# Reordering the start of a linear-attention and bilinear-FFN kernel: unit 0 finished ahead of unit 1, the first up tile by channel tiles, units 2 and 3 one up tile later

## Chip, cores and metric

The kernel runs on one core of a Trainium2 chip. The metric is the device time of one execution in microseconds (us), the median of several runs. Engines are named as in the profile: PE (matrix multiplications), DVE (vector engine), ACT (scalar engine), POOL (GpSimd), and SP, which only issues DMAs here.

## What is computed

A gated linear attention for 4 batches of 8 heads, 768 tokens and 48 channels a head, and behind it a bilinear feed-forward layer on the 3072 tokens of 384 channels:

```python
f = 1.0 / (1.0 + np.exp(-f_logit))
for t in range(S):
    state = f[:, :, t, :, None] * state + np.einsum('bhd,bhe->bhde', k[:, :, t], v[:, :, t])
    y[:, :, t] = np.einsum('bhd,bhde->bhe', q[:, :, t], state)
x = y.transpose(0, 2, 1, 3).reshape(B * S, H * D)
out = ((x @ w_a) * (x @ w_b)) @ w_out          # 384 -> 1536 -> 384
```

## The kernel before

Tokens are cut into 8 blocks of 384 (`BLK`), two a batch. A block's attention is done in two **units** of four heads each; units 0 and 1 (`FIRST`) belong to block 0, units 2 and 3 to block 1, and so on up to 15. What a unit yields goes by DMA into `xT[blk]`, which holds the block's 384 channels as three channel tiles of 128: unit 0 fills channels 0 to 191 (tile 0 and half of tile 1), unit 1 the rest.

A unit runs through these steps, each a function:

- `front_parts(u)` (L313): part 0 is two sigmoids on ACT and one operation on POOL; part 1 two long scans (`scan_f`) and a small `hold` on DVE; part 2 a reciprocal and six short scans (`scan_inv`) on DVE; part 3 the products with `k` and `q` (`times`) on DVE.
- `turn` (transposes of k on PE), `turned` (copies to SBUF on ACT), `scores` (PE), `mask` (DVE), `within` (PE), `gains` (PE), `carried` (five or six small additions on DVE, which make the states `st`), `across` (PE, with the states).
- `out_of_bank` (three copies out of PSUM: part 0 has 128 rows, parts 1 and 2 have 48), `stored` (five DMAs into `xT`), and, for a first half of a batch, `hand_on` (scales the last state for the next block).

Behind that stands the feed-forward layer. For the first two blocks it is done in **up tiles**: `up(blk, ft)` (L598) makes columns 128·ft to 128·ft+127 of both products, b and a, with three matmuls each (one for each channel tile, `kt`), b first, into two of the four PSUM banks `ps_f`; `product` (L624) copies b on ACT and multiplies on DVE into `groups`, which gives the banks back. 12 up tiles a block, 24 in all.

The weights come as 64-bit floats and are converted on the chip in 20 **pieces**: pieces 0 and 1 are w_b and w_a for up tile 0; 2 and 3 those for tiles 1 and 2; 4 and 5 for 3 and 4; 6 and 7 for 5 and 6; 8 and 9 for 7 and 8. A piece costs two ACT operations and one on POOL (`begin`, first half: L71, L72, L73), one more on ACT (`begin`, second half: L75) and, in `end`, one DVE shift (L78) and three DVE additions (L83), one for each channel tile. `begin(9.5)` means: the first half of piece 9 too.

`keep_up(n)` (L1002) issues n matmuls whose result nobody reads.

The order of the work on each engine is written out by hand from L1014 to L1132; behind it a loop runs up tiles alone (L1140), and from L1150 on a planner places everything by estimated costs. [...] Around the change, in the kernel before:

- units 0 and 1 are interleaved: both fronts, then `mask(0)`, `scores(1)`, `within(0)`, `mask(1)`, `within(1)`, then `across(0)`, `across(1)` and the copies of both, and only then the ten DMAs into `xT[0]` (L1062 to L1068). Unit 0's go over SP; of unit 1's, three go over ACT's queue and two over POOL's (L565).
- `keep_up(6)`, `up(0, 0)`, then `turn(2)` and `scores(2)`, `up(0, 1)`, `within(2)`, `gains(2)`, `up(0, 2)`, `across(2)`, `up(0, 3)`, `turn(3)`, `scores(3)`, `up(0, 4)`, `within(3)`, `gains(3)`, `up(0, 5)`, `across(3)`, `y_of(3)`.
- then `ups`: (0, 6), (0, 7), then tiles of block 1 and block 0 in turn. 13 of the remaining 18 run in the loop (`alone`), 5 in the planner's part.
- unit 2's scans and products (L1071, L1082) stand on DVE before pieces 2 and 3, piece 8 is begun and ended before `across(3)`; piece 9 is begun before it, both halves, and ended on DVE in the loop, just ahead of `up(0, 7)`, which needs it.

Of the kernel before, what the change touches and what calls it, by code (L numbers as in the profile page):

```python
# [22 lines left out]
BLK = 384  # L23
# [130 lines left out]
def by_quotients(ctx, tc, q, k, f_logit, v, moe_w_a, moe_w_b, moe_w_out, out, ident, weights, bad, ps_f):  # L154
# [117 lines left out]
    def begin(n):  # L272

        while 2 * n > begun[0] < 2 * len(todo):
            i, second = divmod(begun[0], 2)
            dst, src, shape = todo[i]
            if not second:
                going.append(
                    from_double(
                        nc, dst, raws[i], shape[0], next(blocks), bits[i % len(bits)], some, whole, shape[0] == NKT  # L280
                    )
                    if src.dtype != FP32 else iter(())
                )
            next(going[i], None)
            begun[0] += 1
# [71 lines left out]
            [(DVE, 880, times, "k", inv), (DVE, 880, times, "q", F)],  # L357
        )

    def front(u):  # L360

        for part in front_parts(u):
            for _, _, do, *args in part:
                do(*args)
            yield

    ps_x, ps_y = (ps_a.tile([128, 2, 512], FP32, tag=n, name=n) for n in ("ps_x", "ps_y"))
    idle = list(range(4))

# [113 lines left out]
    def hand_on(u):  # L483

        if unit(u)[1] == NH - 1:
            return
        before = live[u]["st"][-1]
        for n in range(2):
            end = products_of_f[u][:, n, BLK - 1:BLK]
            nc.vector.tensor_scalar(before[:, n], before[:, n], end, math.exp(-MIDDLE), ALU.mult, ALU.mult)  # L490
# [44 lines left out]

    def out_of_bank(u, part):

        if not part:
            if u == NQ - 1:

                live[u]["y_sb"] = groups[:, 2 * NTG - 1, PIECE:].rearrange("r (o p m) -> r o p m", p=2, m=SUB)
            else:
                live[u]["y_sb"] = sb1.tile([128, 2 * NC, 2, SUB], FP32, tag="y", name="y")
        p, e, r, rows = ((0, 0, 0, 128), (1, R, 0, D), (1, 0, R, D))[part]
        copy = nc.vector.tensor_copy if u == NQ - 1 and p else nc.scalar.copy
        copy(live[u]["y_sb"][r:r + rows, :, p], live[u]["y"][p][e:e + rows, 0:BLK].rearrange("r (o m) -> r o m", m=SUB))

    def stored(u):
# [4 lines left out]
    def stores_of(u):  # L553

        b, half, qd = unit(u)
        blk = b * NH + half

        def begin():
            if qd == 0:
                xT[blk] = sb2.tile([128, NKT, BLK], FP32, tag="xT", name="xT")  # L560
            live.pop(u - NQ, None)

        def store(n, h, kt, p, row, w):
            y = live[u]["y_sb"].rearrange("r (n c) p m -> r n (c p m)", n=2)
# [24 lines left out]
    def on_pe(load, do, *args):  # L589
        beats[0] += 1  # L590
        return PE, load, 0, do, *args
# [3 lines left out]

    factors = []

    def up(blk, ft):  # L598

        for _, _, _, do, *args in up_steps(blk, ft):  # L600
            do(*args)

    def up_steps(blk, ft):

        ps = {}

        def emit(nm, w, kt):
            if kt == 0:
                ps[nm] = ps_f[idle.pop(0)]
            nc.tensor.matmul(  # L610
                ps[nm][:, 0:BLK],
                lhsT=w[:, kt, ft * 128:ft * 128 + 128],
                rhs=xT[blk][:, kt],
                start=kt == 0,
                stop=kt == NKT - 1,
            )
            if len(ps) == 2 and kt == NKT - 1:
# [368 lines left out]
    with tc.manual_schedule():  # L986
# [9 lines left out]
        fronts = {u: front(u) for u in (0, 1, 3)}  # L996

        def emit_all(steps):
            for _, _, do, *args in steps:
# [2 lines left out]
        def keep_up(n):  # L1002

            x = products_of_f[0][:, 0]
            for _ in range(n):
                nc.tensor.matmul(ps_f[idle[-1]][:, 0:BLK], lhsT=ident, rhs=x, start=True, stop=True)

        def y_of(u):
            for part in range(3):
                out_of_bank(u, part)  # L1010
            stored(u)

# [1 line left out]
        for u in FIRST:  # L1014
            load_unit(u, "f")
        for u in FIRST:
            next(fronts[u])
        patterns()
        for u in FIRST:
            load_unit(u, "k")  # L1020
# [4 lines left out]
        load_weights(2)  # L1025
        load_unit(2, "k")
        load_unit(2, "q")
        for _ in range(3):
            next(fronts[0])
        begin(1)  # L1030
        keep_up(2)
        turn(0)
        turned(0)
        scores(0)
        begin(2)
        gains(0)
        keep_up(4)
        for _ in range(3):
            next(fronts[1])
        turn(1)  # L1040
        turned(1)
        mask(0)
        scores(1)
        emit_all(front_parts(2)[0])
        begin(2.5)
        carried(0, range(4))
        within(0)
        gains(1, range(NC - 1))
        end(1)
        mask(1)  # L1050

        carried(1, range(1))
        carried(0, range(4, 5))
        _, (first_scan, *scans), *others = front_parts(2)
        emit_all([first_scan])
        within(1)
        gains(1, range(NC - 1, NC))
        across(0)
        carried(1, range(1, NJ))
        carried(0, range(5, NJ))  # L1060
        emit_all(scans)
        for u in FIRST:  # L1062
            if u:
                across(u)
            for part in range(3):
                out_of_bank(u, part)
        for u in FIRST:
            stored(u)  # L1068
        begin(3)
        end(2)  # L1070
        emit_all(others[0])  # L1071
# [8 lines left out]
        keep_up(6)  # L1080
        up(0, 0)
        emit_all(others[1])  # L1082
        begin(4)
        next(fronts[3])
        end(3)
        load_unit(3, "v")
        end(4)
        turn(2)
        scores(2)
        load_unit(4, "f")  # L1090
        up(0, 1)
        mask(2)
        for u in FIRST:
            hand_on(u)
        product()
        turned(2)
        begin(5)
        next(fronts[3])
        next(fronts[3])
        within(2)  # L1100
        gains(2)
        product()
        carried(2)
        begin(6.5)
        up(0, 2)
        across(2)
        end(6)
        next(fronts[3])
        y_of(2)
        load_weights(2)  # L1110
        product()
        begin(7.5)
        up(0, 3)
        turn(3)
        turned(3)
        scores(3)
        end(7)
        mask(3)
        product()
        begin(8)  # L1120
        up(0, 4)
        within(3)
        gains(3)
        end(8)
        carried(3)
        product()
        begin(10)
        end(9)
        up(0, 5)
        across(3)  # L1130
        y_of(3)
        product()  # L1132


        ups = [(0, 6), (0, 7)]
        for i in range(8, NFT):
            ups += [(1, i - 8), (0, i)]
        ups += [(1, i) for i in range(NFT - 8, NFT)]
        alone = len(todo) - 7
        for n, (blk, i) in enumerate(ups[0:alone]):  # L1140
            convert(needed(i))
            up(blk, i)
            end(8 + n)
# [528 lines left out]
```

## Time and profile before

| | |
|---|---|
| median of 3 runs (lowest to highest) | 596.69 us (595.27 to 597.24) |
| the profiled execution's own time, its span | 595.13 us, 593.4 us |
| PE busy, share of the span | 571.1 us, 96% |
| DVE busy | 412.1 us, 69% |
| ACT busy | 256.8 us, 43% |
| chain that ended last | PE 84%, DVE 11% |
| first matmul of any kind | 10.67 us |
| first up matmul starts; the next five of its tile start from | 31.90 us; 34.11 us |
| `across(3)` starts; the next up tile starts | 65.67 us; 66.48 us |

All places in time are counted from the start of the span. "Busy" is time in which an engine worked; what an engine's idle time costs is read from who waited for it.

### The profile page before, as it was taken

What the parts mean: (1) busy time and instruction counts of PE and PEld (TensorE: products, weight loads), DVE (VectorE), ACT (ScalarE), POOL (GpSimd) and SP (SyncE); (2) the same over time, 40 slices, a digit from 0 to 9 for tenths busy, and PEclk for the clock granted to TensorE, in tenths of its full rate; (3) what the DMA queues carried; (4) which work ended last, traced back from release to release, by engine and by line L of the source; (5) the groups of instructions that cost most, each with busy time, mean ns of one, the idle gap of its engine ahead of it and who ended that gap; (6) DMA issues with size and microseconds to landing.
All of it is one profiled execution on the core that took longest, in us unless ns stands there. A gap on an engine that the chain in (4) does not pass through costs nothing.

```text
span 593.4 us, 13932 instructions
## 1 busy us (share of the span) xinstructions
PE 571.1 (96%) x5802; PEld 511.8 (86%) x5802; DVE 412.1 (69%) x786; ACT 256.8 (43%) x487; POOL 89.0 (15%) x72
## 2 busy tenths in 40 slices
PE   2899999999999999999999999999999999999996
PEld 1655655557999999999999999999999999999996
DVE  6999445599978678958895678847785165835751
ACT  5577848653122464235521444326431335135300
POOL 7365637454000000000000000000000000000000
PEclk9999999999999999999999999999999999999999
DMA  8696689089552440044004410041001100000001
GB/s 216 183 253 207 221 263 272 0 150 186 114 144 70 115 93 11 15 119 97 2 1 127 109 22 2 2 106 42 3 1 48 48 2 0 2 28 1 0 29 32
DMA packets 33560, 49.42 MB, mean 83 GB/s; under 512 B 3984, under 2 KB 25264, under 8 KB 33488
## 3 DMA queue, kind: packets, MB, share of 16 engines
q1 hardware_dynamic: 30000, 42.19, 25.8%
q0 software_dynamic: 3056, 5.92, 5.9%
q8 instruction: 47, 0.77, 0.6%
q10 hardware_dynamic: 432, 0.34, 0.2%
q14 instruction: 25, 0.20, 0.1%
HBM read 33.23 MB, written 4.72 MB: 64 GB/s over the span
## 4 chain that ended last, share of the span: by engine, by line
PE 84%; DVE 11%; issue 2%; ACT 1%; DMA 1%; SPq 0%; DVEq 0%; ACTq 0%
PE ps_f L732 35%; PE ps_f L834 28%; PE ps_f L610 13%; PE ps_y L501 2%; DVE inv L346 2%; PE ps_y L527 2%; PE ps_x L403 2%; PE ps_x L452 1%; DVE sums L724 1%; PE ps_x L428 1%; DVE groups L724 1%; DVE w_ba L83 1%; DVE q_in L350 1%; DVE f_in L333 1%; DVE spare L346 1%
## 5 line engine op out<-in xcount | busy, mean ns | idle before, releaser
L610 PE MATMUL ps_f<-xT,w_ba 128*128 128x384 f32 x288 | 95.6, 489 | 1.5 <-DMA xT<-y 1.4
L1319 ACT COPY sums<-ps_f 128x384 f32<-128x384 f32 x120 | 57.5, 480 | 75.8 <-PE ps_f L732 62.2
L610 PEld LDWEIGHTS ps_f<-xT,w_ba 128*128 128x128 f32 x288 | 53.9, 190 | 38.2 <-issue 2.2
L1319 ACT COPY groups<-ps_f 128x384 f32<-128x384 f32 x120 | 57.8, 482 | 64.3 <-PE ps_f L732 41.9
L732 PE MATMUL ps_f<-xT,w_ba 128*128 128x192 f32 x384 | 78.3, 326 | 0.0
L732 PEld LDWEIGHTS ps_f<-xT,w_ba 128*128 128x128 f32 x384 | 64.8, 190 | 0.1
L73 POOL TENSOR_SCALAR sums<-sums 128x768 f32<-128x768 f32 (+1 forms) x20 | 52.2, 2612 | 35.8 <-ACT sums L71 35.6
L732 PE MATMUL ps_f<-groups,w_ba 128*128 128x192 f32 x288 | 55.3, 328 | 0.0
L732 PE MATMUL ps_f<-x_sums,raw 128*128 128x192 f32 x288 | 53.8, 331 | 1.1 <-DVE groups L724 0.9
L329 POOL TENSOR_SCALAR inv<-inv 128x768 f32<-128x768 f32 x14 | 12.9, 923 | 265.9 <-ACT inv L326 265.8
L834 PE MATMUL ps_f<-w_out,sums 128*128 128x192 f32 x288 | 52.1, 329 | 0.3 <-DVE groups L632 0.3
L834 PE MATMUL ps_f<-w_out,groups 128*128 128x192 f32 x288 | 51.7, 328 | 0.0
L732 PEld LDWEIGHTS ps_f<-x_sums,raw 128*128 128x128 f32 x288 | 47.0, 190 | 4.1 <-DVE groups L724 2.1
L834 PE MATMUL ps_f<-spare,sums 128*128 128x192 f32 x288 | 49.0, 326 | 0.0
L732 PEld LDWEIGHTS ps_f<-groups,w_ba 128*128 128x128 f32 x288 | 47.9, 190 | 0.5 <-ACT groups L1319 0.2
L834 PEld LDWEIGHTS ps_f<-w_out,sums 128*128 128x128 f32 x288 | 47.1, 190 | 1.0 <-DVE groups L632 0.6
L834 PEld LDWEIGHTS ps_f<-w_out,groups 128*128 128x128 f32 x288 | 47.1, 190 | 0.7
L834 PEld LDWEIGHTS ps_f<-spare,sums 128*128 128x128 f32 x288 | 47.1, 190 | 0.1
L724 DVE TENSOR_TENSOR sums<-sums,groups 128x768 f32<-128x768 f32 x36 | 34.7, 964 | 13.4 <-ACT groups L1319 13.0
L724 DVE TENSOR_TENSOR sums<-ps_f,sums 128x384 f32<-128x384 f32 x60 | 32.9, 552 | 15.9 <-PE ps_f L732 14.0
L732 PE MATMUL ps_f<-x_sums,w_ba 128*128 128x192 f32 x192 | 39.4, 328 | 0.5 <-DVE sums L724 0.5
L732 PE MATMUL ps_f<-xT,raw 128*128 128x192 f32 x192 | 39.6, 329 | 0.0
(142 smaller groups left out, 851.0 us busy)
## 6 DMA issues: line engine op xcount, KB each, us to landing
raw<-w_ba POOLq DMA_DIRECT2D x11, 512.0 KB, 8.5
k_in<-in_k_dram SPq DMA_DIRECT2D x32, 144.0 KB, 4.4
q_in<-in_q_dram SPq DMA_DIRECT2D x32, 144.0 KB, 4.3
v_in<-in_v_dram SPq DMA_DIRECT2D x16, 288.0 KB, 5.7
raw<-in_moe_w_out_dram SPq DMA_DIRECT2D x6, 768.0 KB, 5.6
out_dram<-o SPq DMA_DIRECT2D x22, 192.0 KB, 1.9
f_in<-in_f_logit_dram SPq DMA_DIRECT2D x28, 144.0 KB, 3.1
xT<-y SPq DMA_DIRECT2D x45, 72.0 KB, 2.1
```

The costliest lines, as they stand in the source:

```text
L73: nc.gpsimd.tensor_scalar(h, h, HI_MIN, HI_MAX, ALU.max, ALU.min)
L83: nc.vector.tensor_tensor(dst[:, rows], hu[:, rows], bit[:, rows], ALU.add)
L329: nc.gpsimd.tensor_scalar(inv, inv, EXP_K, 1.0, ALU.mult, ALU.add)
L346: nc.vector.tensor_tensor_scan(inv[:, w], inv[:, w], none[:, 0:C], first, ALU.mult, ALU.add)
L403: nc.tensor.matmul(ps[h][SUB * p:SUB * p + SUB, o:o + SUB], lhsT=kf[r, tokens(n, c, p)], rhs=qf[r, tokens(n, c, p)], start=True, stop=True,)
L501: nc.tensor.matmul(ps[p][e:e + D, o:o + SUB], lhsT=t["v"][r, n, c, h * D:h * D + D], rhs=at[r, h, o:o + SUB], start=o == 0, stop=True, ski ...
L527: nc.tensor.matmul(ps[p][e:e + D, o:o + SUB], lhsT=st[j][r, n], rhs=qf[r, tokens(n, c, p)], start=False, stop=True, skip_group_check=True,)
L610: nc.tensor.matmul(ps[nm][:, 0:BLK], lhsT=w[:, kt, ft * 128:ft * 128 + 128], rhs=xT[blk][:, kt], start=kt == 0, stop=kt == NKT - 1,)
L724: nc.vector.tensor_tensor(to, x, y, op)
L732: nc.tensor.matmul(ps[:, g], lhsT=sums_of_w[name][:, g, 128 * j:128 * j + 128], rhs=sums_of_x[blk][name], start=start and g == 0, stop=Tru ...
L834: nc.tensor.matmul(to, lhsT=x[:, i // 2, i % 2], rhs=w[:, NI * (i % 2) + i // 2], start=start and i == 0, stop=i == HFT - 1, skip_group_ch ...
L1319: do(*args)
```

## The change

Unit 0 is brought to its end, DMAs included, before unit 1's transposes. Unit 0's states are made between unit 1's short scans. Unit 0's and unit 1's PSUM copies run in the order part 1, part 2, part 0; of unit 1's three, one stays on DVE instead of two. Unit 1's five DMAs into `xT[0]` go round SP, ACT and POOL. `hand_on` for units 0 and 1 moves from four DVE operations to six on ACT. Two `keep_up` calls change from 4 to 3 and from 6 to 3. Up tile 0 goes by channel tiles: b and a of tile 0, then of tile 1, then of tile 2.

On DVE, pieces 2 and 3 move ahead of the second part of unit 2's front (piece 2 ahead of its scans, piece 3 between the scans and the rest). On PE, `up(0, 1)` moves ahead of `turn(2)`, and every later step of units 2 and 3 stands behind one more up tile: `across(3)` now follows `up(0, 6)`. Unit 3's DVE work moves behind `up(0, 3)`. Piece 9 is begun in halves around `y_of(3)`, and ended in the loop. The loop runs 12 up tiles and starts with (0, 7); the planner's part has the same five.

```diff
@@ hand_on
+        if u in FIRST:
+            end = sb2.tile([128, 2], FP32, tag="end", name="end")
+            nc.scalar.mul(end, products_of_f[u][:, :, BLK - 1], math.exp(-MIDDLE))
+            for n in range(2):
+                nc.scalar.mul(before[:, n], before[:, n], end[:, n:n + 1])
+            return
@@ out_of_bank
-        copy = nc.vector.tensor_copy if u == NQ - 1 and p else nc.scalar.copy
+        copy = nc.vector.tensor_copy if u == NQ - 1 and part == 1 else nc.scalar.copy
@@ stores_of
+        queues = itertools.cycle((nc.sync, nc.scalar, nc.gpsimd) if u == NQ - 1 else (nc.sync,))
...
-            queue = nc.sync if u != NQ - 1 else nc.gpsimd if n else nc.scalar
+            queue = next(queues)
@@ up_steps
-        for nm, w in (("b", w_b), ("a", w_a)):
-            for kt in range(NKT):
-                yield on_pe(BEAT, emit, nm, w, kt)
+        order = [(nm, w, kt) for nm, w in (("b", w_b), ("a", w_a)) for kt in range(NKT)]
+        for nm, w, kt in sorted(order, key=lambda x: x[2]) if by_tiles else order:
+            yield on_pe(BEAT, emit, nm, w, kt)
```

The hand-written order in the kernel after, from unit 0's scores on:

```python
        scores(0)
        *scans, hold = parts[1][1]
        emit_all(scans)
        mask(0)
        emit_all([hold])
        begin(2)
        gains(0, range(NC - 1))
        emit_all(parts[2][0])
        within(0)
        gains(0, range(NC - 1, NC))
        keep_up(3)
        for i, step in enumerate(parts[1][2]):
            emit_all([step])
            if i > 1:
                carried(0, range(i - 2, i - 1))
        across(0)
        emit_all(parts[1][3])
        turn(1)
        y_of(0)
        turned(1)
        scores(1)
        end(1)
        mask(1)
        begin(2.5)
        gains(1, range(NC - 1))
        within(1)
        gains(1, range(NC - 1, NC))
        carried(1, range(NJ - 1))
        across(1)
        y_of(1)
        for u in FIRST:
            carried(u, range(NJ - 1, NJ))
        end(2)
        begin(3)
...
        keep_up(3)
        up(0, 0, True)
        begin(4)
        end(3)
        load_unit(3, "v")
        emit_all(parts[2][1])
        end(4)
        load_unit(4, "f")
        emit_all(parts[2][2])
        emit_all(parts[2][3])
        emit_all(parts[3][0])
        up(0, 1)
        product()
        for u in FIRST:
            hand_on(u)
        begin(5)
        turn(2)
        scores(2)
        turned(2)
        up(0, 2)
        end(5)
        mask(2)
        product()
        begin(6)
        within(2)
        gains(2)
        end(6)
        up(0, 3)
...
        up(0, 6)
        product()
        carried(3)
        across(3)
        begin(9.5)
        end(9)
        y_of(3)
        begin(10)
        product()

        ups = [(0, 7), (0, 8), (1, 0), (1, 1), (1, 2)]
...
        alone = len(todo) - 8
        for n, (blk, i) in enumerate(ups[0:alone]):
            convert(needed(i))
            up(blk, i)
            end(8 + n + n // 6)
```

More of the change, by code (lines that the diff above doesn't have):

```diff
@@ L358, in front_parts @@
         )
[L360 to L365, printed above, removed]
     ps_x, ps_y = (ps_a.tile([128, 2, 512], FP32, tag=n, name=n) for n in ("ps_x", "ps_y"))
@@ L536, in out_of_bank @@
     def out_of_bank(u, part):
-        if not part:
+        if "y_sb" not in live[u]:
             if u == NQ - 1:
@@ L596, in by_quotients, with up, up_steps @@
     factors = []
-    def up(blk, ft):
-        for _, _, _, do, *args in up_steps(blk, ft):
+    def up(blk, ft, by_tiles=False):
+        for _, _, _, do, *args in up_steps(blk, ft, by_tiles):
             do(*args)
-    def up_steps(blk, ft):
+    def up_steps(blk, ft, by_tiles=False):
         ps = {}
@@ L616, in emit @@
             )
-            if len(ps) == 2 and kt == NKT - 1:
+            if nm == "a" and kt == NKT - 1:
                 factors.append((blk, ft, ps))
-        for nm, w in (("b", w_b), ("a", w_a)):
-            for kt in range(NKT):
-                yield on_pe(BEAT, emit, nm, w, kt)
+        order = [(nm, w, kt) for nm, w in (("b", w_b), ("a", w_a)) for kt in range(NKT)]
+        for nm, w, kt in sorted(order, key=lambda x: x[2]) if by_tiles else order:
+            yield on_pe(BEAT, emit, nm, w, kt)
     def product():
@@ L995, in by_quotients @@
             nc.scalar.copy(ps[:, :, 0:BLK], zero.unsqueeze(1).broadcast_to((128, 2, BLK)))
-        fronts = {u: front(u) for u in (0, 1, 3)}
+        parts = {u: front_parts(u) for u in range(2 * NQ)}
         def emit_all(steps):
@@ L1008, in y_of @@
         def y_of(u):
-            for part in range(3):
+            for part in (1, 2, 0) if u in FIRST else range(3):
                 out_of_bank(u, part)
@@ L1016, in by_quotients @@
         for u in FIRST:
-            next(fronts[u])
+            emit_all(parts[u][0])
         patterns()
@@ L1027, in by_quotients @@
         load_unit(2, "q")
-        for _ in range(3):
-            next(fronts[0])
+        for part in parts[0][1:]:
+            emit_all(part)
         begin(1)
@@ L1034, in by_quotients @@
         scores(0)
+        *scans, hold = parts[1][1]
+        emit_all(scans)
+        mask(0)
+        emit_all([hold])
         begin(2)
[L1036 to L1039, printed above, removed]
+        gains(0, range(NC - 1))
+        emit_all(parts[2][0])
+        within(0)
+        gains(0, range(NC - 1, NC))
[4 more added lines that the diff above has]
+                carried(0, range(i - 2, i - 1))
+        across(0)
+        emit_all(parts[1][3])
         turn(1)
+        y_of(0)
         turned(1)
-        mask(0)
         scores(1)
[L1044 to L1048, printed above, removed]
         end(1)
         mask(1)
[L1052 to L1055, printed above, removed]
+        begin(2.5)
+        gains(1, range(NC - 1))
         within(1)
         gains(1, range(NC - 1, NC))
[L1058 to L1061, printed above, removed]
+        carried(1, range(NJ - 1))
+        across(1)
+        y_of(1)
         for u in FIRST:
[L1063 to L1068, printed above, removed]
+            carried(u, range(NJ - 1, NJ))
+        end(2)
         begin(3)
-        end(2)
-        emit_all(others[0])
         load_unit(3, "f")
@@ L1079, in by_quotients @@
         load_unit(3, "q")
-        keep_up(6)
-        up(0, 0)
-        emit_all(others[1])
+        keep_up(3)
+        up(0, 0, True)
         begin(4)
-        next(fronts[3])
         end(3)
         load_unit(3, "v")
+        emit_all(parts[2][1])
         end(4)
+        load_unit(4, "f")
+        emit_all(parts[2][2])
+        emit_all(parts[2][3])
+        emit_all(parts[3][0])
+        up(0, 1)
+        product()
+        for u in FIRST:
+            hand_on(u)
+        begin(5)
         turn(2)
         scores(2)
-        load_unit(4, "f")
-        up(0, 1)
+        turned(2)
+        up(0, 2)
+        end(5)
         mask(2)
-        for u in FIRST:
-            hand_on(u)
         product()
[L1096 to L1099, printed above, removed]
+        begin(6)
         within(2)
         gains(2)
+        end(6)
+        up(0, 3)
+        carried(2)
+        across(2)
         product()
[L1103 to L1108, printed above, removed]
+        load_weights(2)
+        for part in parts[3][1:3]:
+            emit_all(part)
+        begin(8)
         y_of(2)
-        load_weights(2)
+        up(0, 4)
+        emit_all(parts[3][3])
         product()
-        begin(7.5)
-        up(0, 3)
         turn(3)
+        scores(3)
         turned(3)
-        scores(3)
-        end(7)
+        end(8)
+        up(0, 5)
+        product()
         mask(3)
-        product()
-        begin(8)
-        up(0, 4)
+        begin(9)
         within(3)
         gains(3)
-        end(8)
+        up(0, 6)
+        product()
         carried(3)
-        product()
[L1127 to L1139, printed above, removed]
+        across(3)
+        begin(9.5)
+        end(9)
+        y_of(3)
+        begin(10)
+        product()
+        ups = [(0, 7), (0, 8), (1, 0), (1, 1), (1, 2)]
+        for i in range(9, NFT):
+            ups += [(0, i), (1, i - 6)]
+        ups += [(1, i) for i in range(NFT - 6, NFT)]
+        alone = len(todo) - 8
         for n, (blk, i) in enumerate(ups[0:alone]):
@@ L1142, in by_quotients @@
             up(blk, i)
-            end(8 + n)
+            end(8 + n + n // 6)
             product()
```

## The prediction

> **What bounds the kernel now.** First the waits of PE over the whole span, in total, times and longest:
>
> ```profile
> PE ps_f L1006 <- POOL ident masks.py:199: 10.7, 1, 10.7
> PE ps_f L610 <- DMA xT<-y: 1.4, 1, 1.4
> PE ps_x L527 <- DVE st L481: 0.9, 1, 0.9
> ```
>
> PE hardly waits after its first matmul: the kernel is PE work behind a start. The change makes the same useful matmuls, so what counts is how much PE idles or runs `keep_up` before PE is full. PE's timeline says when that is:
>
> ```profile
> 34.11 3.46 PE L610 MATMUL ps_f<-xT,w_ba 128*128 128x384 f32 x10 [1.40 <-DMA xT<-y]
> ...
> 49.40 1.17 PE L527 MATMUL ps_x<-q_in,st 48*48 48x64 f32 x48 [0.92 <-DVE st L481]
> 50.71 4.11 PE L610 MATMUL ps_f<-xT,w_ba 128*128 128x384 f32 x12
> ```
> ```profile
> 66.48 63.48 PE L610 MATMUL ps_f<-xT,w_ba 128*128 128x384 f32 x196
> ```
>
> From 50.71 on PE is full; the last line is 63 us of up tiles without a gap. By stage (columns: stretch, length, busy us and instructions of PE, weight loads, DVE, ACT, POOL, clock, DMA):
>
> ```profile
> 15.00:30.00 15.00, 12.83 (x389) 10.19 (x382) 13.78 (x34) 8.17 (x15) 5.20 (x4) 1.00 0.62 178
> 30.00:45.00 15.00, 13.60 (x175) 8.54 (x174) 14.63 (x30) 11.49 (x15) 10.38 (x8) 1.00 0.95 259
> 60.00:75.00 15.00, 15.00 (x177) 9.25 (x176) 6.43 (x17) 13.42 (x18) 10.35 (x4) 1.00 0.65 223
> ```
>
> DVE is the full engine from 15 to 50 us, and idle half the time behind it. So in the start every round trip that leaves DVE idle is lost. Last, ACT and DVE around the end of unit 3:
>
> ```profile
> 66.64 1.46 ACT L546 COPY y<-ps_y 128x384 f32<-128x384 f32 x3 [1.28 <-PE ps_y L527]
> 68.13 1.07 ACT L630 COPY x_sums<-ps_f 128x384 f32<-128x384 f32 x2
> ...
> 71.19 0.55 DVE L78 TENSOR_SCALAR sums<-sums 128x768 uint32<-128x768 uint32 x1
> 71.77 1.10 DVE L83 CUSTOM_DVE_ANT_0 w_ba<-sums,spare 128x512 uint16<-128x512 uint16 x3
> 72.25 5.82 PEld L610 LDWEIGHTS ps_f<-xT,w_ba 128*128 128x128 f32 x19 [0.31 <-DVE w_ba L83]
> ```
>
> L83 at 71.77 is piece 9. Its L75 ran at 64.20, before the copies; even so the weight loads of `up(0, 7)` waited 0.31 us for it, with `up(0, 6)` in between.
>
> [...] the b copy at 68.13 starts when the y copies ahead of it end. [...] Here the first four records take 2.93 us, later eight take 2.85; no later drop shows. [...] L350 on q at 34.41 took 1.58 us beside POOL's L73, 0.95 at 53.73 without, but L83 at 50.14 took 1.10 beside one[...]. [...] The trace: 0.6 us an issue, 2.0 / 2.9 / 3.4 us (least, median, most) to landing in `xT`.
>
> **The change, step by step**, by durations of the profile of before.
>
> *Unit 0.* `scores(0)` ends at 16.2 as before. `mask(0)` 0.95 to 17.2; DVE has waited 0.7 for it. The first state addition waits for the last `gains`, which stands behind `within`: 0.7 + 0.4, so 18.3. Then five pairs of short scan (0.31 to 0.42) and addition (0.16), 2.6 us: 21.0; products with k and q 1.75: 22.7. `across(0)` and unit 0's copies (1.46) go beside these; its five DMAs issue on SP from 23.3, where SP was idle from 17.5 to 28.0. They land long before use: nothing.
>
> *Unit 1.* `scores(1)` to 23.7, mask to 24.65, `within` and last `gains` 1.1 to 25.8, five chained additions 1.39 to 27.2, first half of `across(1)` 0.7 to 28.0. DVE copy 0.57 to 28.55; ACT's two wait for it, 0.96, to 29.5; two issues on ACT 1.2; then L75 of piece 2, 1.16, to 31.9. DVE, with an addition pair and piece 1 (1.0) to do, idles about 1.2 + 0.8 + 1.4 us here. This is what bringing one unit to its end alone costs: nothing of the other fills the round trips.
>
> *Up tile 0.* `keep_up(3)`, 2.07 us, from 28.8 to 30.9; two matmuls 1.36 to 32.2; tile 1 lands at 29.5 + 3.0, tile 2 at 30.1 + 3.4; the end is 35.2, against 37.4 before: 2.2 gained. `up(0, 1)`: b to 37.2, a behind piece 3.
>
> *Unit 2's front behind pieces 2 and 3.* L83 of piece 2 1.1 to 33.05; two scans and `hold` 2.0 to 35.1; L73 of piece 3 on POOL from 32.8 takes 2.77 to 3.56, so L78 starts at 36.0; L78 and L83 2.0 to 38.0 (1.7 to 2.3); scans 2.3, k 0.9, q 0.95 to 1.58: 42.5. `scores(2)` 0.86 ends at about T = 43.5 (bounds 42.5 to 44.6). PE has ended `up(0, 1)` at 39.3 and waits 2.1 us for k, then for q. Before, `scores(2)` and `up(0, 1)` were both done at 43.01: the 2.2 us are gone, given to the front.
>
> *From T to the end of unit 3.* Five up tiles of 4.07, turn and scores 1.44, twice within and gains 1.34, twice across 0.82 (the chain of waits) are 26.1. Before: 27.6 from 38.94, as PE waited 0.92 for unit 2's states and that `across` ran slow. After, product, piece 4, mask, product, piece 5 are on DVE by 49 while `up(0, 3)` runs to 53, so states come in time. I find no wait over 0.3 us; the tightest is `up(0, 5)` on pieces 6 and 7, which stand behind unit 3's whole front (margin 0.4 to 0.8). I take 0.3 for it, bounds 0 to 1. So `across(3)` ends at 69.6 + 0.3. Before, with one tile more, 66.5 + 4.07 = 70.55: 0.65 gained.
>
> *Piece 9.* Here I see the loss. `up(0, 7)` follows `across(3)` at once (end E). Its a half needs L83 of piece 9. ACT: y copies from E + 0.08, 1.49; L75, queued behind them, 1.02; b copy of `up(0, 6)` 0.48: E + 3.1. DVE: the product of `up(0, 6)`, ahead of piece 9, 0.47; L78 0.58; first L83 0.5: E + 4.65. The b half lasts 2.0. PE waits 2.65 us (2.4 to 2.9). What the wait brings late behind it (pieces 10 and 11, needed three tiles later) has room.
>
> *Other edits.* `hand_on` on ACT: six operations[...]; piece 4 behind it is needed 5 us later than it comes. DVE is free of 0.93 (four operations) after T: nothing. Four `keep_up` matmul pairs fewer: they stood in idle time. The order of the planner's part doesn't change but for banks, so its gaps stay.
>
> *Sum.* −0.65 + 2.65 = +2.0 us. The profiled execution has 595.13 (span 593.4 and 1.7 around it): 597.1. It lies 1.56 under the median shown, 596.69, so on that basis 598.7.
>
> **Rivals.**
>
> *The front isn't late (not slower).* Place: the end of q's product in unit 2's front. Price: each us that it ends before 42.5 is a us less, down to 39.3 + 1.44 = 40.7 for T, where PE never waits: 2.8 less, 595.9, and with no wait at `up(0, 5)` 595.6; with earlier landing of `xT`, 594. It decides from T = 41.5 on. For it: q's product ended at 36.0 before; pieces 2 and 3 add 3.4 to 4.6, a copy less takes 0.6 off, so DVE without the new waits would be there at 39 to 40. Against it: the three waits on unit 1, each a chain of named operations.
>
> *Still later.* If L73, L83 and q take their upper values and `up(0, 5)` waits 1 us: T = 44.6, +3.8, so 600.5. For it: DMA and POOL are full from 30 to 45 us.
>
> *PE's clock falls.* PE idles 2 us before `turn(2)` and 2.65 at `up(0, 7)`. [...] Against it: [...] the clock was 1.00 in each stage.
>
> *A later gap closes.* PE's 2.2 us of waits after 130 us could move with DVE's phase: 594.5. Nothing in the change touches them.
>
> **Chances.** What can be told from no change is 0.3%, 1.8 us. Forecast 0.52 (own range 597.3 to 600), 0.31 of it slower by more and 0.21 within; front not late 0.24 (0.14 faster, 0.10 within); still later 0.15 and clock 0.05, slower; later gap 0.04, faster. Faster 0.18, same 0.31, slower 0.51. The range takes in the upper rivals and most of the first one: 595.3 to 600.9.
>
> **What would show it.** In the timeline after: `up(0, 0)` ends near 35; PE waits some 2 us for L350 on k ahead of unit 2's transposes; `scores(2)` ends at 43.5; `across(3)` near 70; a wait of 2.65 us on L83 in the up tile behind it, with L75 behind three y copies on ACT. I am wrong if PE isn't idle there, if `scores(2)` ends before 41.5, or if the clock row shows a dip.

## The result and the profile after

The kernel after takes 602.84 us (median of 6 runs, 601.66 to 605.43), the kernel before, run beside it, 595.77 (6 runs, 595.27 to 597.24): ratio 1.0118, 95% interval 1.0095 to 1.0141. It is slower by 7.1 us, where 2.0 were forecast. Its profiled execution takes 603.39 us with a span of 601.7, against 595.13 and 593.4.

The three longest of PE's waits in the kernel after, behind its first matmul (in total, times, longest):

```profile
PE ps_f L611 <- DVE w_ba L83: 3.0, 1, 3.0
PE ps_y L421 <- DVE k_in L350: 1.4, 1, 1.4
PE ps_y L526 <- DVE st L474: 1.3, 1, 1.3
```

The wait on DMA that stood at the first up tile before (1.4 us) is gone; in its place are waits on DVE. Where they lie, in PE's timeline of the kernel after:

```profile
27.84 1.42 PE L526 MATMUL ps_y<-q_in,st 48*48 48x64 f32 x40 [1.27 <-DVE st L474]
30.39 4.21 PE L1007 MATMUL ps_f<-groups,ident 128*128 128x384 f32 x6 [1.13 <-DVE st L474]
34.38 8.41 PE L611 MATMUL ps_f<-xT,w_ba 128*128 128x384 f32 x24
44.15 0.77 PE L421 MATMUL ps_y<-ident,k_in 112*128 112x112 f32 x6 [1.35 <-DVE k_in L350]
...
45.78 4.14 PE L611 MATMUL ps_f<-xT,w_ba 128*128 128x384 f32 x12
...
71.87 2.20 PE L611 MATMUL ps_f<-xT,w_ba 128*128 128x384 f32 x6
77.07 13.28 PE L611 MATMUL ps_f<-xT,w_ba 128*128 128x384 f32 x31 [2.99 <-DVE w_ba L83]
```

The second line is the thing to look at: six records of `keep_up` (a matmul of this size shows as two records) take 4.21 us, where 12 took 4.14 in the kernel before. PE runs at half speed there (clock 0.50). The stages say so too (stretch, length, busy us and instructions of PE, weight loads, DVE, ACT, POOL, then PE's clock, DMA share, GB/s), kernel after:

```profile
25.00:30.00 5.00, 2.73 (x111) 2.27 (x104) 1.92 (x7) 1.28 (x3) 2.77 (x1) 0.86 0.24 64
30.00:35.00 5.00, 4.61 (x7) 2.52 (x8) 4.42 (x11) 3.48 (x5) 2.11 (x3) 0.50 0.49 123
...
80.00:85.00 5.00, 5.00 (x11) 2.71 (x11) 0.56 (x1) 1.49 (x3) 1.53 (x1) 0.68 1.02 289
```

The clock was 1.00 in all three stretches before. It falls twice, from 28.56 to 35.39 and from 76.35 to 83.18 us (worked out from stretches of 0.5 us), 6.83 us each. From 30 to 35 us PE is "busy" 4.61 us with 7 instructions: busy time alone hides this.

A yardstick for the whole start is a matmul of the planner's part that waits 0.46 us in either kernel (first the kernel before, then the kernel after):

```profile
227.96 0.92 PE L732 MATMUL ps_f<-x_sums,w_ba 128*128 128x192 f32 x4 [0.46 <-DVE sums L724]
```
```profile
235.62 0.92 PE L733 MATMUL ps_f<-x_sums,w_ba 128*128 128x192 f32 x4 [0.46 <-DVE sums L725]
```

It comes 7.66 us later, of the 8.3 us by which the span is longer: nearly all of the loss has happened by then. At the up tile behind `across(3)` the kernel after is 71.87 − 70.55 = 1.32 us late (70.55 is the time of before for the same work, from the prediction); then PE waits 2.99; behind that it loses 3.35 more. 1.32 + 2.99 + 3.35 = 7.66.

Most of the 3.35 is the clock. The same 178 records behind the same wait, first in the kernel after, then in the run with the moved stop (told below), where the clock didn't fall:

```profile
77.07 60.68 PE L611 MATMUL ps_f<-xT,w_ba 128*128 128x384 f32 x178 [2.99 <-DVE w_ba L83]
```
```profile
78.30 57.67 PE L611 MATMUL ps_f<-xT,w_ba 128*128 128x384 f32 x178 [2.99 <-DVE w_ba L83]
```

So this fall costs 3.01 us (half of the 6.11 us from 77.07 to 83.18 would be 3.05). The remaining 0.34 is not traced to its end; a stop of PE further on, with no wait shown, is 0.25 us longer here (0.79 at 157.61) than in the kernel before (0.54 at 149.81).

The wait of 2.99 is made as forecast. ACT, then DVE, around the end of unit 3 in the kernel after:

```profile
72.03 1.46 ACT L545 COPY y<-ps_y 128x384 f32<-128x384 f32 x3 [5.12 <-PE ps_y L526]
73.52 1.15 ACT L75 ACTIVATE spare<-raw,some 128x768 f16<-128x768 f32 x1
74.54 0.45 ACT L631 COPY x_sums<-ps_f 128x384 f32<-128x384 f32 x1
```
```profile
75.03 0.56 DVE L633 TENSOR_TENSOR groups<-ps_f,x_sums 128x384 f32<-128x384 f32 x1 [4.65 <-ACT x_sums L631]
...
76.09 1.59 DVE L83 CUSTOM_DVE_ANT_0 w_ba<-sums,spare 128x512 uint16<-128x512 uint16 x3
```

L75, written behind the three y copies, starts at 73.52, just as they end (72.03 + 1.46 = 73.49). Both engines idled for about 5 us before (5.12, 4.65), while piece 9 could have been converted.

### The profile page after: what moved, and what is told of

The parts are those of the page before. It is cut to its first block, busy times and chain, and to the rows that moved or that the text cites. A ratio compares the mean times of both kernels' runs of the same rounds, so it can differ in the third digit from the quotient of the medians.

```text
span 601.7 us, 13917 instructions
## 1 busy us (share of the span) xinstructions
PE 573.9 (95%) x5794; PEld 512.3 (85%) x5794; DVE 414.5 (69%) x781; ACT 257.5 (43%) x494; POOL 90.4 (15%) x71
## 4 chain that ended last, share of the span: by engine, by line
PE 86%; DVE 6%; issue 3%; ACT 2%; POOL 2%; DMA 1%; SPq 0%; DVEq 0%; ACTq 0%; POOLq 0%
PE ps_f L733 35%; PE ps_f L835 28%; PE ps_f L611 14%; PE ps_x L396 2%; PE ps_y L500 2%; PE ps_y L526 2%; PE ps_x L445 1%; DVE sums L725 1%; DVE inv L346 1%; PE ps_x L421 1%; POOL sums L73 1%; DVE groups L725 1%; DMA f_in<-in_f_logit_dram 1%; PE ps_f L1007 0%; DVE k_in L350 0%
## 5 line engine op out<-in xcount | busy, mean ns | idle before, releaser
L611 PE MATMUL ps_f<-xT,w_ba 128*128 128x384 f32 x288 | 99.1, 503 | 3.0 <-DVE w_ba L83 3.0
L611 PEld LDWEIGHTS ps_f<-xT,w_ba 128*128 128x128 f32 x288 | 55.8, 197 | 41.7 <-DVE w_ba L83 4.2
L733 PEld LDWEIGHTS ps_f<-xT,w_ba 128*128 128x128 f32 x384 | 64.8, 190 | 0.1
```

The source lines that it names most:

```text
L611: nc.tensor.matmul(ps[nm][:, 0:BLK], lhsT=w[:, kt, ft * 128:ft * 128 + 128], rhs=xT[blk][:, kt], start=kt == 0, stop=kt == NKT - 1,)
L733: nc.tensor.matmul(ps[:, g], lhsT=sums_of_w[name][:, g, 128 * j:128 * j + 128], rhs=sums_of_x[blk][name], start=start and g == 0, stop=Tru ...
```

## The experiments

Two questions were put: does the loss come from the waits alone, or from the clock that they let fall; and does the start or the later order cost the time? Every ratio is to the kernel before, run beside.

**Piece 9 early.** `end(10)` ahead of unit 3's copies.

```diff
         end(9)
-        y_of(3)
         begin(10)
+        end(10)
+        y_of(3)
         product()
```

> Edit: piece 9 is converted to its end (L75 on ACT, L78 and L83 on DVE) ahead of unit 3's copies instead of behind them, where ACT and DVE are idle. Theory A (the wait of 3.0 us costs itself and, by letting the clock fall, some 3.2 us more, as 15 records take 8.12 us instead of 5.1): wait and second clock fall both go, 602.8 - 6.2 = 596.6 us, ratio to before about 1.001 to 1.003, clock 1.00 from 70 to 90 us. Theory B (only the wait counts; the clock falls for another reason, such as the load of PE): 602.8 - 3.0 = 599.8 us, ratio about 1.007, and the clock still falls near 77 us.

Measured: 598.49 us, ratio 1.0049 (1.0035 to 1.0062): between the two. The profiled execution is the slowest of the six (601.32); PE's timeline in it:

```profile
45.74 1.12 PE L421 MATMUL ps_y<-ident,k_in 112*128 112x112 f32 x6 [1.95 <-DVE k_in L350]
...
48.29 6.38 PE L611 MATMUL ps_f<-xT,w_ba 128*128 128x384 f32 x12
...
76.62 13.81 PE L611 MATMUL ps_f<-xT,w_ba 128*128 128x384 f32 x42
```

The last line runs on without a wait and at full clock (42 records in 13.81 us, 0.33 us each; 31 in 13.28 in the kernel after): wait and fall at piece 9 are gone. But the clock fell at 46.01, behind a wait of 1.95 us for unit 2's k, where it had not fallen in the kernel after. So a fall isn't tied to one place. The other five executions have mean clocks of 0.989 to 0.994, so falls stayed in them too.

**Filling the wait.** Four matmuls that nobody reads, between the b and the a half of `up(0, 7)`; piece 9 as late as in the kernel after.

```diff
+                emit_all(x[1:] for x in steps[0:NKT])
+                fill(4)
+                emit_all(x[1:] for x in steps[NKT:])
```

> Edit: four extra matmuls of 128x384 that nobody reads, 2.8 us at full clock, between the b and the a half of up(0, 7), where PE waits 3.0 us; piece 9 comes as late as in the kernel after. Theory A (PE's idleness lets the clock fall): no fall near 77 us, 602.8 - 3.2 = 599.6 us, ratio about 1.0065. Theory B (the clock falls for another reason than the idle time): the wait is filled, nothing is gained, 602.8 us or a little more, ratio about 1.012, clock at half near 77 us.

Measured: 601.15 us, 1.0103 (1.0083 to 1.0122). The timeline:

```profile
74.86 2.74 PE L1012 MATMUL ps_x<-xT,ident 128*128 128x384 f32 x8
78.02 12.20 PE L611 MATMUL ps_f<-xT,w_ba 128*128 128x384 f32 x37 [0.42 <-DVE w_ba L83]
```

The clock stays at 1.00 there, where the kernel after had 0.50 from 76.35 on, though PE did more work (2.74 us of it): in this pair of executions its idleness let the clock fall, not its load. (On the grid told below, the stretch from 74.05 to 77.46 would have been busy for about 1 us without the fill, by an estimate; with it PE was busy throughout.) The median alone doesn't separate this run from the kernel after, as their intervals overlap. In the profiled execution the start came 0.95 us later (the tile behind `scores(2)` at 46.73), 0.56 of it by a stop that the next run shows; yet at the yardstick it is 233.64, 1.98 us ahead of the kernel after. From the a half of `up(0, 7)` on (78.02 against 77.07) it gains 2.93, about what the fall costs.

**Filling the start.** Two such matmuls ahead of `across(1)` and two behind it.

```diff
         carried(1, range(NJ - 1))
+        fill(2)
         across(1)
+        fill(2)
```

> Edit: two extra matmuls of 128x384 ahead of across(1) and two behind it, in PE's idle times of 1.27 and 1.13 us there. Theory A1 (the first clock fall, 28.5 to 35.5 us, costs what it takes from PE, half of 6.5 us): no fall, 602.8 - 3.2 = 599.6 us, ratio about 1.0065. Theory A2 (it is mostly covered, as PE waits for unit 2's k on DVE at 44.15 us anyway; only the second half of across(1) and what hangs on it came later by it): clock 1.00 from 25 to 40 us, PE waits over 3 us for k instead of 1.35, the up tile behind scores(2) starts at 45.2 instead of 45.78, gain 0.3 to 0.9 us, about 602.2 us, ratio about 1.011. Theory B (the load of PE lets the clock fall): it still falls near 28 us and nothing is gained.

Measured: 604.33 us, 1.0144 (1.0128 to 1.016), if anything slower than the kernel after, with which its interval overlaps. None of the theories had this:

```profile
27.50 0.39 PE L445 MATMUL ps_f<-v_in,kT 64*48 64x48 f32 x2 [2.22 <-issue]
27.82 2.91 PE L1012 MATMUL ps_x<-groups,ident 128*128 128x384 f32 x4
30.66 1.15 PE L526 MATMUL ps_y<-q_in,st 48*48 48x64 f32 x40
```

PE stands still for 2.22 us in the midst of unit 1's last gains, with no wait shown. Counted in the program, the stop lies behind the 180th matmul. It is there in the kernel before as well (0.19 us, inside `across(0)`) and in the kernel after (0.26), and its length differs from execution to execution. In this order unit 1's states hang on it. The filling matmuls then ran at half clock (2.91 us) and kept `across(1)` waiting, which started at 30.66 instead of 27.84.

**Both** (early piece 9, four matmuls round `across(1)`).

> Edit: the early piece 9 and the four extra matmuls round across(1), together. Theory A with A2: 602.8 - 6.2 - 0.6 = 596.0 us, ratio 1.000 to 1.002, clock 1.00 all over. With A1: 593.4 us, ratio 0.996. Theory B: 599.8 us.

Measured: 598.44 us, 1.0048 (1.0031 to 1.0065), again between the theories. In the median the fills add nothing to the early piece 9: in the profiled execution the start ran at full clock, but the clock fell at 44.38, behind a wait of 2.35 us for unit 2's k. The six executions split by their mean clock: 597.08 to 597.49 us at 0.998 to 1.000, and 599.38 to 600.12 at 0.993 to 0.996. The same program meets a fall in some executions and not in others, and is some 2 to 3 us slower where it does.

Laid beside each other, the falls of these profiles and of the later ones (15 in nine kernels) show a grid. (Falls at the very end of the program, when PE's work is done, are left out.) Each lasts 3.41 or 6.83 us, and in one execution they start whole multiples of 3.41 us apart by the trace's record of the clock: 14.00, 5.00, 6.00 and 16.00, 2.00, and 14.00 of them in the five executions with more than one. The rise to full clock at the start (14.91 in the kernel after) lies on the same grid, 2.00, 3.00, 4.00 or 9.00 stretches ahead of the first fall. In the stretch of 3.41 us ahead of a fall PE was busy for 0.54 to 1.95 us (busy times by the same view as below). Counted from the start of the span, where the grid lies differs from execution to execution: the first falls stand 0.0 to 3.3 us behind a multiple of 3.413. And a stretch need not be idle for PE's clock to fall behind it: 1.95 us busy, some half of it, was still little enough.

**Moving the stop.** One keep_up matmul fewer ahead of `across(0)`, in the kernel after.

```diff
         gains(0, range(NC - 1, NC))
-        keep_up(3)
+        keep_up(2)
```

> Edit: one keep_up matmul fewer ahead of across(0) (3 becomes 2), nothing else. In every profile so far PE stands still behind the 180th matmul of the program with no wait shown, for 0.19 us in the kernel before and 0.26, 0.82, 1.07, 1.41 and 2.22 us in the kernel after and its variants; in the kernel before it falls into across(0), in the kernel after ahead of the last matmul of unit 1's last gains, on which unit 1's states and all behind them wait. Theory A (the stop belongs to the place in the program and costs its whole length in the kernel after): it now falls between the gains and across(1), where PE waits 1.27 us for states anyway; gain about 1 us against the kernel after, 601.8 us, ratio about 1.010; the wait behind gains x14 is gone. Theory B (it belongs to these gains, by what they read): it stays ahead of the last gains' last matmul, ratio about 1.012. Both clock falls may stay.

Measured: 601.04 us, 1.0089 (1.0074 to 1.0104). The last gains run without a stop, so it belongs to the place in the program (in the run without falls, below, it shows right behind them). How much it costs can't be read from this, since another thing changed in the profiled execution. The clock fell twice in the start (22.27 and 29.10); but at the wait for piece 9, 2.99 us as in the kernel after, it didn't. PE by the grid's stretches (length, busy us and instructions, clock, DMA share, GB/s), first the kernel after, then this one:

```profile
72.94:76.35 3.41, 1.14 (x4) 1.00 0.16 46
76.35:79.77 3.42, 2.70 (x4) 0.50 0.58 172
79.77:83.18 3.41, 3.41 (x7) 0.50 0.94 296
```
```profile
73.46:76.88 3.42, 1.86 (x6) 1.00 0.13 36
76.88:80.29 3.41, 1.99 (x6) 1.00 0.44 128
```

In the kernel after, 2.27 us of the wait lie in one stretch; here a border cuts it into 1.57 and 1.42, and the two stretches are busy for 1.86 and 1.99 us instead of one for 1.14. The same wait costs 3 us or 6 (2.99, or 2.99 + 3.01), by where the grid happens to lie.

**A shorter wait.** In the kernel after, L75 of piece 9 alone moves ahead of the copies.

> Edit: in the kernel after, only L75 of piece 9 moves ahead of unit 3's copies; its end stays in the loop. PE's wait in up(0, 7) becomes 1.6 us (product of up(0, 6), L78 and the first L83 behind the copies) instead of 3.0. Theory A (the clock falls where a stretch of a fixed 3.41 us grid has PE busy for 1.9 us or less): a wait of 1.6 us leaves 1.8 us only if it lies whole in one stretch, about half the executions; so 1.4 us gained in all of them and 3.3 us more in half, two groups of times, ratio about 1.0068 in the middle. Theory B (an idle time as such lets the clock fall, from some length on, whatever its place): one group, at 1.0095 if 1.6 us is long enough or at 1.004 if it isn't. The fall in the start may stay, and spreads both.

Measured: 601.10 us, 1.0081 (1.005 to 1.0112). The wait was 2.00 us, not 1.6. The seven executions lie at 597.27, 597.27 and 599.02, and at 601.10 to 603.35. That is the wide spread of Theory A rather than the one group of Theory B, but seven don't show two groups: the gap between them (2.08) is hardly wider than one inside the lower (1.75), and falls in the start spread them too. In the profiled execution, of the upper ones, the clock fell at 77.10, behind a stretch with 1.41 us busy.

**No falls.** Early piece 9, matmuls into all of PE's waits of the start, stop moved.

```diff
-        up(0, 1)
+        emit_all(x[1:] for x in steps[0:NKT])
+        fill(2)
+        emit_all(x[1:] for x in steps[NKT:])
...
+        fill(3)
         turn(2)
```

> Edit: early piece 9; two extra matmuls ahead of across(1), two behind it, two between the halves of up(0, 1), three ahead of unit 2's transposes; one keep_up matmul fewer ahead of across(0). In the profiles so far the clock fell at the end of a stretch of 3.41 us of a fixed grid in which PE was busy for 1.9 us or less (0.57 to 1.89 in nine falls), and not where it was busy for 2.05 or more. Theory A: no such stretch is left, clock 1.00 all over; across(1) starts near 27.0 us, unit 2's k is ready 16.05 us behind it as in the runs with a full clock, the up tile behind scores(2) starts at 44.5, and with 26.1 us to the end of unit 3 and no wait behind it the time is that of before + 0.1, 595.4 us (594.6 to 596.5), ratio 0.999 to 1.002. Theory B (what is left is in the order on DVE and in the later tiles, clock and stop cost little): as the run with both fills, ratio 1.004 to 1.006.

Measured: 597.10 us, 1.0025 (1.0013 to 1.0037), between the two theories, and in the profiled execution the clock is 1.00 all over. The timeline:

```profile
26.84 1.56 PE L1012 MATMUL ps_x<-groups,ident 128*128 128x384 f32 x4 [1.47 <-issue]
28.32 1.15 PE L526 MATMUL ps_y<-q_in,st 48*48 48x64 f32 x40
...
45.97 4.14 PE L611 MATMUL ps_f<-xT,w_ba 128*128 128x384 f32 x12
...
72.06 8.33 PE L611 MATMUL ps_f<-xT,w_ba 128*128 128x384 f32 x25
```

The late piece 9 and the clock made up most of the loss: 1.0118 is down to 1.0025. What is left is the start: the stop (now 1.47 us, ahead of the fill) and the fill behind it let `across(1)` start at 28.32 instead of 27.0, unit 2's transposes start at 44.33, 16.0 us later, and 26.1 us after 45.97 unit 3 ends, at 72.06, which is 1.5 behind the kernel before. In the kernel after the same 16.0 would give 43.85 for the transposes, against 44.15: by this estimate the first fall, 6.83 us long, cost only 0.3 us there, since DVE was late anyway.

**The old start with the later order.** The kernel before up to `up(0, 1)`, then the order of the kernel after, with the early piece 9.

> Edit: the kernel before up to scores(2) and up(0, 1), and from there the order of the kernel after, with the early piece 9. It leaves out the reordered start (units 0 and 1, tile order of the first up tile, pieces 2 and 3 ahead of unit 2's front). Theory A (the start loses, the later order by itself gains): scores(2) and up(0, 1) end at 43.0 as before, 26.1 us more to the end of across(3), 69.1 against 70.55 for the same work in the kernel before: 1.4 us faster than before, ratio 0.9975. Theory B (units 2 and 3 a tile later bring nothing, or waits for pieces 4 to 7 take it): ratio 1.000 or above.

Measured: 594.97 us, 0.9986 (0.9971 to 1.0001). The up tile behind `across(3)` starts at 69.40 (70.55 before), the yardstick at 227.09 (227.96). This doesn't show that the later order by itself gains anything: the interval reaches 1, and in the profiled execution the start, whose code is that of before, was already 0.66 us early (`up(0, 1)` from 38.28 instead of 38.94). From there to the tile behind `across(3)` the gain is 0.5 us where 1.4 was expected; one wait is left:

```profile
59.03 4.21 PE L610 MATMUL ps_f<-xT,w_ba 128*128 128x384 f32 x12 [0.56 <-DVE w_ba L83]
...
69.40 20.91 PE L610 MATMUL ps_f<-xT,w_ba 128*128 128x384 f32 x64
```

What the pair of runs does show is the start: this one and the run without falls (1.0025) have the same later order and the early piece 9, and differ by 0.39%, some 2.3 us, in favour of the old start.

**The front between the pieces.** The reordered start as in the run without falls, but on DVE unit 2's scans stand ahead of piece 2 and the rest of its front ahead of piece 3, and on PE unit 2's transposes and scores stand between the halves of `up(0, 1)`.

```diff
+        emit_all(parts[2][1])
         end(2)
...
+        emit_all(parts[2][2])
+        emit_all(parts[2][3])
         end(4)
```

> Edit: as the run without falls (early piece 9, extra matmuls round across(1), one keep_up fewer), but on DVE unit 2's scans stand ahead of piece 2 and the rest of its front ahead of piece 3, and on PE the b half of up(0, 1), two extra matmuls, unit 2's transposes and scores, then the a half. Theory A (the lateness of unit 2 comes from pieces 2 and 3 standing ahead of its front, in which DVE first waits for ACT): the scans fill DVE's wait, q and k are ready near 39, scores(2) and up(0, 1) are done at 42.7 against 44.5 of the run without falls, so 593.5 us, ratio 0.997 (0.995 to 0.999). Theory B (DVE's amount of work sets the time, not its order): done at 44.5, ratio 1.000.

Measured: 597.79 us, 1.0038 (1.0024 to 1.0051), above both theories. Unit 2's transposes started at 40.45 instead of 44.33, without a wait for k: the order on DVE does set when k is ready. But the gain was given back at the next step, where the mask stood behind piece 4:

```profile
50.52 0.89 PE L500 MATMUL ps_x<-at,v_in 64*48 64x64 f32 x48 [2.19 <-DVE at L409]
```

**The mask ahead of piece 4**, on top of that (`mask(2)` ahead of `end(5)`).

> Edit: as the run with the front between the pieces, but mask(2) on DVE stands ahead of piece 4 instead of behind it; there PE waited 2.19 us for the mask ahead of within(2), and DVE 4.07 us for POOL ahead of piece 4. Theory A (the reordered start, freed of clock falls and of the late front, is as good as the old start and no better): the wait of 2.19 us goes, across(3) ends at 71.2 against 73.36, 0.6 behind the kernel before (70.55 with the same work), ratio 1.000 to 1.002. Theory B (piece 4's lateness takes the wait's place, at up(0, 3)): ratio stays at 1.003 to 1.004.

Measured: 597.93 us, 1.0043 (1.0028 to 1.0059). That wait went, but the profiled execution had a fall at 22.85 and three waits of 0.5 to 0.6 us further on. The ratio is that of Theory B, though the wait at `up(0, 3)` was only 0.47 us; whether the reordered start could be brought level with the old one stays open.

**The old start, filled.** On top of the old start with the later order: `up(0, 0)` by channel tiles, and unit 3's two scans in DVE's idle times ahead of pieces 4 and 5.

```diff
-        up(0, 0)
+        up(0, 0, True)
...
         up(0, 2)
+        emit_all(third[1][0:1])
         end(5)
...
+        emit_all(third[1][1:2])
         end(6)
         up(0, 3)
```

> Edit: the old start with the later order, and two changes more: up(0, 0) by channel tiles, and unit 3's two long scans put on DVE into its idle times of 1.01 and 1.23 us ahead of pieces 4 and 5. Theory A (with the old start the later order leaves PE waiting only for xT's second tile, 1.23 us, and for piece 6, 0.56 us, which is late because unit 3's scans stand ahead of it): 0.55 us less at the first, 0.13 and 0.56 us less at turn(3) and up(0, 5): across(3) ends near 68.2 against 69.40, ratio 0.9965 (0.995 to 0.998). Theory B (POOL and the loads of the pieces set the time there, so that a filled DVE gains nothing): as the run with the old start, 0.9986.

Measured: 594.39 us (22 runs), 0.9985 (0.9974 to 0.9997), the ratio of Theory B. This version is clearly faster than the kernel after; against the one before, its interval lies just below 1 (by 0.2 to 1.5 us), and it is the best of eleven versions, so the gain is small if it is one. That it is faster than the run with the old start alone is not shown. The waits of 1.23, 0.13 and 0.56 us don't show any more, but the profiled execution had a fall at 25.00, and `across(3)` ended no earlier (the tile behind it at 69.38).

## Why the prediction was wrong

**Unit 0.** Right: its products end with q at 22.80 (21.86 + 0.94), forecast 22.7.

**Unit 1 and unit 2's front (T).** Too early: T was put at 43.5 with bounds 42.5 to 44.6, and the tile behind `scores(2)` starts at 45.78, outside them. The terms: `across(1)` starts some 0.6 late (27.84), 0.26 of it the stop. Its copy on DVE waits for the whole of it, 1.15 at full clock and 1.42 here, not for half (0.7). ACT's two issues took 1.43 for 1.2. And DVE's operations ran longer beside POOL's than the rows taken from quieter stretches. DVE, then POOL, in the kernel after:

```profile
37.42 1.17 DVE L78 TENSOR_SCALAR sums<-sums 128x768 uint32<-128x768 uint32 x1
38.72 1.49 DVE L83 CUSTOM_DVE_ANT_0 w_ba<-sums,spare 128x512 uint16<-128x512 uint16 x3
```
```profile
37.44 0.74 POOL L231 MEMSET f_in<- 128x768 f32 x1
38.26 1.02 POOL L329 TENSOR_SCALAR spare<-spare 128x768 f32<-128x768 f32 x1
```

At 45.26 and 45.94, with POOL idle from 43.92 to 46.97, the same two take 0.55 and 1.10. That POOL is the cause was not tried by itself, and L83 has run at 1.10 beside it too (50.14 in the kernel before). The scans took 2.42 for 2.0, the short ones 2.9 for 2.3. From L83 of piece 2 to k's end I had 9.25 us, measured 10.35 (33.65 to 44.00). From k to T it was 0.5 less than forecast (1.78 for 2.3), as q is ready by the time the transposes are done.

**Up tile 0.** Forecast to end at 35.2; it only starts at 34.38, since `keep_up(3)` started at 30.39 instead of 28.8 and took 4.21 us at half clock. This cost nothing more, as PE waited for k until 44.15 anyway.

**From T to the end of unit 3.** Right: 71.87 − 45.78 = 26.09, forecast 26.1, and the 0.3 for `up(0, 5)` wasn't needed. So at `across(3)` the forecast of −0.65 became +1.32, all of it from T.

**Piece 9.** Right in place and cause; 2.99 for 2.65, just over the bounds (2.4 to 2.9). On ACT the chain kept to the forecast. What it had too short is L83: its three operations take 1.59 us here, 1.10 in the kernel before, and the first, on which PE waits, 0.93 instead of 0.42. Why is open.

**`hand_on`.** Its six operations take 1.5 us on ACT (38.69 to 40.18). Piece 4 behind them came in time, as forecast: PE's only wait on a converted piece is the one on piece 9 (3.0 us, once).

**The clock.** This is the step that failed: the sum has no term for a fall of the clock, and one came. Without its 3.0 us the time would be about 599.8 (an estimate: 602.84 − 3.01), inside the range. The rival "PE's clock falls" had a chance of 0.05; against it stood that "the clock was 1.00 in each stage". It came true twice: at the wait of 2.99 us, which left PE busy for 1.14 us of the stretch ahead of the fall, and in unit 1, where the stop of 0.26 us and a wait of 1.27 among small matmuls left it busy for 1.89. The fall at piece 9 cost 3.01 us. The clock of before was no argument against it: the profile of before has no fall until 593.41, when PE's work is done, and so couldn't show what lets the clock fall. What counts in these runs isn't the length of one idle time but how much PE works in a fixed stretch of 3.41 us, with a limit near half of it: the clock fell behind stretches with up to 1.95 us busy, and behind none with 2.01 or more. By that the forecast's own 2.65 us of idle time at piece 9 would have been priced with a fall in a good part of the executions (an estimate: where it lies whole in one stretch, 3.41 − 2.65 = 0.76 us are left). Its last sign of being wrong, a dip in the clock row, is the one that came.

**Sum.** Forecast +2.0; at the yardstick +7.66, made up of 1.97 more at T, 0.34 more at piece 9, and 3.35 behind it, 3.01 of them for the clock. That the result is slower was right, and late piece 9 was its place; but the fall that follows on the wait, which the sum left out, costs as much again as the wait, and T, the second miss, lay beyond its bound.

## What to carry to other kernels

Price an idle time of PE by how much of a fixed stretch of 3.41 us it leaves empty: in these runs the clock fell where PE was busy for 0.54 to 1.95 us of one, and then 3.41 or 6.83 us at half speed followed, which at piece 9 cost as much as the wait itself (3.01 us, 2.99). Before a step is put right behind another, look at what it needs and start that in the idle time ahead; moving one conversion ahead of three copies brought 4 us (602.84 to 598.49). When PE's waits are filled with matmuls that nobody reads, the fill must be shorter than the wait, since the next step stands behind it: two such matmuls took 2.91 us at half clock where the kernel after waits 1.27.

## What was not expected of the hardware

- The clock's grid, as told above. Its limit isn't one number of busy time: behind the twelve stretches with 0.54 to 1.65 us busy the clock fell, behind those with 2.01 or more it didn't; in between it fell at 1.89 (twice) and 1.95, and didn't at 1.70, 1.86 and 1.99 (moved stop), 1.91 (the front between the pieces), 1.95 (no falls) and 1.68 (filling the wait, near the end). In most of those that didn't fall PE had worked on matmuls of 112 or 128 rows, while in those that fell at 1.89 and 1.95 it had mostly worked on the small ones of the attention. Whether size counts was not tried.
- The kernel before isn't free of falls: its mean clock was between 0.990 and 1.000 over its runs, and a fall at the very end of the program takes at most some 0.003 of it (3.08 us at half clock in the kernel after, from 598.59 on).
- PE's stop behind the 180th matmul, with no wait shown: 0.19 to 2.22 us, at the same place of the program in both kernels. Beside it the traces show this: the list of DMA queues has one of the kind "instruction" (47 packets, 0.77 MB), and in all nine profiles that show the stop one of its packets of 16 KB lands 1.26 to 1.52 us before the stop ends (at 25.22 and 26.63 in the kernel before, 25.02 and 26.29 in the kernel after), though the end itself lies anywhere from 26.29 to 27.50. The stop near 150 us has such a packet 1.28 to 1.53 us before its end in all 13 profiles (148.38 and 149.81 in the kernel before, 156.14 and 157.61 in the kernel after). Whether PE waits for it was not tried.
